# Convolution and leaky-ReLU feed-forward on one core: w_in fetched once, wider first transposes, fewer warm-ups, weight and x on two queues

## The chip, the cores and the metric

The kernel runs on one core of a Trainium2 chip. The metric is the device time of one execution in microseconds (us).

The profile names the engines PE (TensorE), PEld (its weight loads), DVE (VectorE), ACT (ScalarE), POOL (GpSimd) and SP (SyncE).

## The reference

```python
w = exp(weight - max); w = w / (sum(w) + 1e-9)            # 8 heads, 7 taps
out[b, s, h*24 + g] = sum_k w[h, k] * x_pad[b, s + k, h*24 + g]   # causal, 6 zeros ahead
h = out.reshape(32768, 192) @ moe_w_in                    # 192 x 2048
g = maximum(0.01 * h, h)
return g @ moe_w_out                                      # 2048 x 192, float32
```

## The kernel before

The 192 channels are three chunks of 64. Two batch rows lie side by side in the partitions (e = 0 in 0 to 63, e = 1 in 64 to 127), so the kernel keeps each weight that multiplies them in both halves. The work goes in groups: the first eight have 256 columns, the others 512. A group is convolved ("yt"), multiplied by w_in into PSUM ("ph", the first product), passed through leaky ReLU by ScalarE ("g"), and multiplied by w_out ("po" or "acc", the second product). The second product of a group runs one group later, so group 0 has no second product beside it.

The first 1024 columns of x do not take the usual path through DMA transposes, whose load and transpose take a median of 3.2 and 3.9 us from issue to landing in this kernel's profile. They are loaded in four quarters and transposed on TensorE: quarter 0 comes as float32 over the sync queue (`x_nat`), is cast, transposed into PSUM, the memory that this kernel's matmuls write ("ptr"), and evacuated, that is copied out, into `xt`; quarters 1 and 2 (`x_rows`) come over GpSimd's queue.

```python
def load_w_in(n, e):                       # six transfers: 3 pieces x 2 halves
    fs = slice(pieces[n] * 128, pieces[n + 1] * 128)
    nc.gpsimd.dma_start(out=w_in[n][e * CH : (e + 1) * CH],
                        in_=moe_w_in[:, fs].rearrange("(c p) f -> p c f", p=CH))
...
load_w_in(0, 0); make_identity(nc, ident); load_w_in(0, 1)
for e in range(2): load_w_in(1, e)
load_first(1)                              # x_rows, quarter 1
for e in range(2): load_w_in(2, e)
load_first(2)
nc.gpsimd.dma_start(out=w_out..., in_=moe_w_out...)
```

In group 0, chunks 0 and 1 are convolved on TensorE with diagonal weights (`diag`, each tap as a high and a low bfloat16 part, p = 0 and 1), chunk 2 on VectorE. In group 1, TensorE does chunk 0 and VectorE the other two. Idle TensorE time in the prologue is filled with matmuls on zeros ("warm").

## Time and profile before

| | |
|---|---|
| time, first three runs | 687.36 to 687.89 us, median 687.63 |
| span of the profiled run | 685.2 us (that run: 687.25 us) |
| first convolution on TensorE | 6.57 to 10.4 us |
| first product in earnest | from 10.95 us |
| second product | from 22.25 us |
| w_out's transfer | issued 9.64, landed 22.2 us |

Read it from the last row but one: TensorE waits for nothing from the second product's first matmul to the end (the waits view names no PE wait after 22.25 us, and PE is busy 200.00 of the 200 us from 200 to 400). The lines behind the table stand in the prediction.

### The profile page before, as it was taken

How to read it: one execution, taken by the hardware profiler on the slowest of the kernel's cores; microseconds unless marked ns; L12 is line 12 of the kernel's file. 1: busy time of each engine (PE TensorE's matmuls, PEld its weight loads, DVE VectorE, ACT ScalarE, POOL GpSimd, SP SyncE). 2: the span in 40 equal slices, each digit the busy share in tenths (PEclk: the TensorE clock that was granted, in tenths of full speed). 3: DMA queues.
4: the chain of work that ended last, by engine and by line, in shares of the span. 5: the costliest groups of instructions: out<-in, count | busy, mean ns of one | idle time of the engine just before them, and what ended most of it. 6: DMA issues, size and time to landing. Idle time of an engine off the chain costs nothing.

```text
span 685.2 us, 27404 instructions
## 1 busy us (share of the span) xinstructions
PE 679.2 (99%) x12572; PEld 466.0 (68%) x12572; DVE 483.7 (71%) x851; ACT 524.6 (77%) x623; POOL 147.5 (22%) x206
## 2 busy tenths in 40 slices
PE   9999999999999999999999999999999999999998
PEld 6899987666666666666666666666666666666667
DVE  6889668567687667786677786676876676876612
ACT  7888898777777778777777777777777778777781
POOL 7732222222102222022222022221122220000000
PEclk9999999999999999999999999999999999999999
DMA  9986658466566565575574565574665664321123
GB/s 155 112 96 95 83 70 107 44 76 89 84 87 76 55 83 85 82 95 68 55 91 80 87 87 67 60 95 75 90 81 61 72 91 75 72 55 34 34 49 93
DMA packets 211699, 53.88 MB, mean 79 GB/s; under 512 B 204288, under 2 KB 211200, under 8 KB 211584
## 3 DMA queue, kind: packets, MB, share of 16 engines
q0 software_dynamic: 99536, 14.76, 30.5%
q1 hardware_dynamic: 112048, 37.38, 26.9%
q8 instruction: 98, 1.61, 0.9%
q14 instruction: 17, 0.14, 0.1%
HBM read 29.88 MB, written 25.17 MB: 80 GB/s over the span
## 4 chain that ended last, share of the span: by engine, by line
PE 95%; DMA 2%; POOL 1%; ACT 1%; issue 0%; DVE 0%; POOLq 0%
PE ph L406 47%; PE acc L495 41%; PE po L432 7%; DMA w_out<-in_moe_w_out_dram 2%; ACT g L413 1%; POOL w_in L251 1%; POOL x_rows L125 0%; POOL sel L236 0%; DVE o_sb L543 0%; POOL ident masks.py:199 0%; POOL sel L234 0%; POOL ident masks.py:197 0%; PE ptr L151 0%; POOLq masks.py:199 0%; POOLq L642 0%
## 5 line engine op out<-in xcount | busy, mean ns | idle before, releaser
L413 ACT ACTIVATE g<-ph 128x1024 bf16<-128x1024 f32 x512 | 496.3, 1021 | 136.3 <-PE ph L406 135.8
L195 DVE SCALAR_TENSOR_TENSOR yt<-xt,wk,yt 128x512 bf16<-128x512 bf16 (+1 forms) x630 | 388.2, 696 | 0.2
L406 PE MATMUL ph<-yt,w_in 64*64 64x512 bf16 (+2 forms) x6048 | 377.9, 363 | 1.4 <-ACT g L413 0.7
L495 PE MATMUL acc<-g,w_out 64*64 64x512 bf16 x5184 | 316.5, 376 | 0.0
L406 PEld LDWEIGHTS <-w_in 64*64 64x64 bf16 (+1 forms) x6048 | 237.7, 129 | 98.9 <-issue 3.9
L495 PEld LDWEIGHTS <-w_out 64*64 64x64 bf16 x5184 | 166.3, 118 | 110.5
L80 POOL DMA_DIRECT2D x_bf<-in_x_dram x180 | 134.2, 779 | 412.3 <-DMA xt<-x_bf 408.4
L517 DVE STREAM_TRANSPOSE o_t<-acc 128x512 f32<-128x512 f32 x81 | 68.1, 884 | 170.0 <-PE acc L495 170.0
L432 PE MATMUL po<-w_out,g 64*128 64x192 bf16 (+1 forms) x1152 | 59.7, 243 | 0.2 <-DMA w_out<-in_moe_w_out_dram 0.2
L432 PEld LDWEIGHTS <-g 64*128 64x128 bf16 (+1 forms) x1152 | 55.2, 94 | 2.0 <-issue 0.8
L189 DVE TENSOR_SCALAR yt<-xt,wk 128x512 bf16<-128x512 bf16 (+1 forms) x105 | 29.4, 333 | 12.8 <-DMA xt<-x_bf 9.0
L505 ACT COPY junk<-junk 128x1 f32<-128x1 f32 x54 | 10.3, 191 | 3.9
L543 ACT COPY o_sb<-po 128x192 f32<-128x192 f32 x32 | 10.1, 320 | 1.5 <-PE po L432 0.2
L543 DVE COPY o_sb<-po 128x192 f32<-128x192 f32 x8 | 2.8, 356 | 6.8 <-PE po L432 3.8
L170 DVE COPY xt<-ptr 128x384 bf16<-128x384 bf16 x7 | 2.2, 353 | 6.0 <-PE ptr L158 3.2
L286 PE MATMUL warm<-zero 128*128 128x256 bf16 (+1 forms) x20 | 4.8, 404 | 1.1 <-DVE junk L231 1.1
L214 PE MATMUL acc<-xt,diag 64*64 64x256 bf16 x84 | 5.5, 288 | 0.0
L214 PEld LDWEIGHTS <-diag 64*64 64x64 bf16 x84 | 4.7, 115 | 0.9 <-DVE rsum L366 0.4
L129 POOL DMA_DIRECT2D x_half<-in_x_dram x6 | 4.3, 713 | 3.2 <-DMA w_in<-in_moe_w_in_dram 3.2
L251 POOL DMA_DIRECT2D w_in<-in_moe_w_in_dram x6 | 3.9, 656 | 0.0
L286 PEld LDWEIGHTS <-zero 128*128 128x128 bf16 x20 | 2.5, 136 | 2.1 <-DVE junk L231 1.1
L347 ACT ACTIVATE diag<-ident,whm 128x64 bf16<-128x64 bf16 x14 | 3.5, 336 | 0.0
(41 smaller groups left out, 18.8 us busy)
## 6 DMA issues: line engine op xcount, KB each, us to landing
out_dram<-o_t SPq DMA_DIRECT2D x108, 192.0 KB, 4.6
x_bf<-in_x_dram POOLq DMA_DIRECT2D x180, 64.0 KB, 3.2
out_dram<-o_sb SPq DMA_DIRECT2D x16, 192.0 KB, 3.0
xt<-x_bf SPq DMA_TRANSPOSE x90, 3.9
w_in<-in_moe_w_in_dram POOLq DMA_DIRECT2D x4, 192.0 KB, 5.4
w_in<-in_moe_w_in_dram POOLq DMA_DIRECT2D x2, 384.0 KB, 8.5
w_out<-in_moe_w_out_dram POOLq DMA_DIRECT2D x1, 768.0 KB, 12.6
out_dram<-o_sb SPq DMA_DIRECT2D x8, 96.0 KB, 1.9
```

The source lines that it names most:

```text
L80: nc.gpsimd.dma_start(out=t[:, c, :, e, :], in_=src[2 * rp + e, :, :, c * CH : (c + 1) * CH],)
L189: lambda s=src, d=dst, c=c: nc.vector.tensor_scalar_mul(d, s, wk[:, c, 0:1])
L195: lambda s=src, d=dst, c=c, k=k: nc.vector.scalar_tensor_tensor(out=d, in0=s, scalar=wk[:, c, k : k + 1], in1=d, op0=mybir.AluOpType.mult, ...
L214: lambda k=k, p=p, a=a, e=e, ps=ps: nc.tensor.matmul(out=acc[ps, :T], lhsT=diag[c][ps, p, k, :], rhs=xt[0][ps, c, a : a + T], start=(k == ...
L251: nc.gpsimd.dma_start(out=w_in[n][e * CH : (e + 1) * CH], in_=moe_w_in[:, fs].rearrange("(c p) f -> p c f", p=CH),)
L406: nc.tensor.matmul(out=ph[m : m + M, e, i * T : (i + 1) * T], lhsT=w_in_of(f, ps, c, m, m + M), rhs=y[ps, c, t0 : t0 + T], start=(c == 0), ...
L413: act = nc.scalar.activation(out=g[blk][:, nf * u : nf * (u + 1), :, t0 : t0 + T], in_=ph.rearrange("p e (i t) -> p i e t", i=nf), func=my ...
L432: return nc.tensor.matmul(out=po[m], lhsT=g[b][ps, fc, e, s * 128 : (s + 1) * 128], rhs=w_out[ps, fc, :], start=start, stop=stop,)
L495: ins = nc.tensor.matmul(out=acc2[gi, r][e * CH : (e + 1) * CH, 0:T], lhsT=w_out_of(ps, fc, r), rhs=g[b][ps, fc, e, t0 : t0 + T], start=fi ...
L505: seal = nc.scalar.copy(out=junk, in_=junk)
L517: nc.vector.transpose(out=osb[gi, 0][:, 0 : T // GB, :, r], in_=acc2.pop((gi, r))[:, 0:T].rearrange("p (j k) -> p j k", k=GB),)
L543: ins = copy(out=o_sb[:, n % 2, :], in_=po.pop(n))
```

## The change

Its intent is a shorter prologue. w_in is fetched once: 128 of its 192 rows land over all partitions, the other 64 in the lower half, and VectorE copies what the other half lacks (`spread_down`, `spread_up`). Chunk 2 of group 0 goes to TensorE too, with input and output halves crossed, so that its matmuls run beside those of the others. The first transposes take all 128 partitions. The weight is issued from ScalarE's queue so that x goes first on the sync queue. The casts of quarter 0 are shared between ScalarE and VectorE, as its evacuations were before. Of the warm-ups, nine of 256 columns between the weight's matmuls and the convolution become one of 256 and one of 512, and the nine of 256 and one of 128 at the start become six of 512.

```diff
-    NPEC = 2
+    NPEC = 3
...
+        t = psum_o.tile([128, HS, NCH, 128], BF16, name="ptr", tag="po")   # one PSUM tile, was two
+        for s in range(HS):
+            for c in range(NCH):
+                if q == 0:
+                    nc.tensor.transpose(out=t[:, s, c, :], in_=x_half[q][:, c, s, :, :]..., identity=ident)
...
-    nc.sync.dma_start(out=w9[:, 0:K], in_=weight)
+    nc.scalar.dma_start(out=w9[:, 0:K], in_=weight)
...
+    def load_w_in(n, rows):
+        ps, slot = ((0, 128), 0) if rows == 0 else ((0, CH), 2)
+        nc.gpsimd.dma_start(out=w_in[n][ps[0] : ps[1], slot],
+                            in_=moe_w_in[rows : rows + ps[1], n * WF : (n + 1) * WF])
+    def spread_down(n):
+        nc.vector.tensor_copy(out=w_in[n][0:CH, 1, :], in_=w_in[n][CH:128, 0, :])
+    def spread_up(n):
+        nc.vector.tensor_copy(out=w_in[n][CH:128, 1:3, :], in_=w_in[n][0:CH, 0:3:2, :])
...
-    warm(9)
-    warm(1, 128)
+    warm(6, ST)
...
-    warm(6)
+    warm(1)
...
-    warm(3)
+    warm(1, ST)
...
-    for e in range(2):
-        cast_first(0, e, nc.scalar.copy)
+    cast_first(0, 0, nc.scalar.copy)
+    cast_first(0, 1, nc.vector.tensor_copy)
...
+    run(pe_0[:K])
+    run(pe_0[K:], pe_2[:K])
+    evac_0(act_scale)
+    run(pe_1[:K], pe_2[K:])
+    evac_2(nc.vector.tensor_scalar_mul)
+    run(pe_1[K:])
+    evac_1(act_scale)
...
-                    evac_y(act_scale)          # group 1's TensorE chunk: ScalarE, at once
+                evac_0(nc.vector.tensor_scalar_mul)   # now VectorE, at the end of group 0
```

More of the change, by code (lines that the diff above doesn't have):

```diff
@@ L2 @@
 from contextlib import ExitStack
+from itertools import zip_longest
 import concourse.bass as bass
@@ L142, in transpose_first @@
     def transpose_first(q):
-        ts = [
-            psum_o.tile([128, HS, NCH, CH], BF16, name=f"ptr{i}", tag="po") for i in range(2)
-        ]
-        for s in range(HS):
-            for c in range(NCH):
-                for i in range(2):
-                    ps = slice(i * CH, (i + 1) * CH)
-                    if q in x_half:
+        if q == 3:
+            ts = [
+                psum_o.tile([128, HS, NCH, CH], BF16, name=f"ptr{i}", tag="po")
+                for i in range(2)
+            ]
+            for s in range(HS):
+                for c in range(NCH):
+                    for i in range(2):
+                        ps = slice(i * CH, (i + 1) * CH)
                         nc.tensor.transpose(
@@ L155, in transpose_first @@
                         )
-                        continue
-                    for e in range(2):
-                        nc.tensor.transpose(
-                            out=ts[i][e * CH : (e + 1) * CH, s, c, :],
-                            in_=x_rows[q][ps, e, s, c * CH : (c + 1) * CH],
-                            identity=ident[ps, ps],
-                        )
-        ptr[q] = ts
-    def evac_first(q, *copies):
-        dst = xt[0][:, :, HALO + q * HT : HALO + (q + 1) * HT].rearrange(
-            "p c (s i k) -> p i s c k", s=HS, i=2
-        )
-        for i, t in enumerate(ptr.pop(q)):
-            copies[i](out=dst[:, i], in_=t)
+            ptr[q] = ts
+            return
+        t = psum_o.tile([128, HS, NCH, 128], BF16, name="ptr", tag="po")
+        for s in range(HS):
+            for c in range(NCH):
+                if q == 0:
+                    nc.tensor.transpose(
+                        out=t[:, s, c, :],
+                        in_=x_half[q][:, c, s, :, :].rearrange("p e k -> p (e k)"),
+                        identity=ident,
+                    )
+                    continue
+                for e in range(2):
+                    nc.tensor.transpose(
+                        out=t[e * CH : (e + 1) * CH, s, c, :],
+                        in_=x_rows[q][:, e, s, c * CH : (c + 1) * CH],
+                        identity=ident,
+                    )
+        ptr[q] = t
+    def evac_first(q, *copies):
+        dst = xt[0][:, :, HALO + q * HT : HALO + (q + 1) * HT]
+        t = ptr.pop(q)
+        if q == 3:
+            dst = dst.rearrange("p c (s i k) -> p i s c k", s=HS, i=2)
+            for i in range(2):
+                copies[i](out=dst[:, i], in_=t[i])
+            return
+        dst = dst.rearrange("p c (s k) -> p s c k", s=HS)
+        for s in range(HS):
+            copies[s](out=dst[:, s], in_=t[:, s])
     yt = {}
@@ L200, in conv_jobs, with pe_conv_jobs @@
         return jobs
-    def pe_conv_jobs(grp, c, parts=(0, 1)):
+    def pe_conv_jobs(grp, c, parts=(0, 1), cross=False):
         blk, t0, T = grp
@@ L210, in pe_conv_jobs @@
                 a = BASE + k + blk * ST + t0
+                both = []
                 for e in range(2):
                     ps = slice(e * CH, (e + 1) * CH)
-                    jobs.append(
-                        lambda k=k, p=p, a=a, e=e, ps=ps: nc.tensor.matmul(
-                            out=acc[ps, :T], lhsT=diag[c][ps, p, k, :],
+                    to = slice((e ^ cross) * CH, ((e ^ cross) + 1) * CH)
+                    both.append(
+                        lambda k=k, p=p, a=a, ps=ps, to=to: nc.tensor.matmul(
+                            out=acc[to, :T], lhsT=diag[c][ps, p, k, :],
                             rhs=xt[0][ps, c, a : a + T],
@@ L220, in pe_conv_jobs, with evac, run @@
                     )
-        return jobs, lambda scale: scale(yt[blk][:, c, t0 : t0 + T], acc[:, :T], rsum[:, c, :])
+                jobs.append(both)
+        def evac(scale):
+            if blk not in yt:
+                yt[blk] = yt_pool.tile([128, NCH, ST], BF16, name="yt")
+            y = yt[blk][:, c, t0 : t0 + T]
+            if not cross:
+                scale(y, acc[:, :T], rsum[:, c, :])
+                return
+            for e in range(2):
+                ps = slice(e * CH, (e + 1) * CH)
+                frm = slice((1 - e) * CH, (2 - e) * CH)
+                scale(y[ps], acc[frm, :T], rsum[frm, c, :])
+        return jobs, evac
+    def run(*lists):
+        for slots in zip_longest(*lists, fillvalue=()):
+            for both in slots:
+                for job in both:
+                    job()
     w9 = const_pool.tile([H, K + 1], FP32, name="w9")
-    nc.sync.dma_start(out=w9[:, 0:K], in_=weight)
+    nc.scalar.dma_start(out=w9[:, 0:K], in_=weight)
     load_first(0)
-    zero = const_pool.tile([128, HT], BF16, name="zero")
-    nc.vector.memset(zero, 0.0)
+    ones = nc.const_aps.tensor(1.0, [128, ST], BF16)
     junk = const_pool.tile([128, 1], FP32)
@@ L240, with w_in_of @@
         )
-    pieces = (0, NFC // 4, NFC // 2, NFC)
-    w_in = [
-        const_pool.tile([128, NCH, (b - a) * 128], BF16, name=f"w_in{a}")
-        for a, b in zip(pieces[:-1], pieces[1:])
-    ]
-    def load_w_in(n, e):
-        fs = slice(pieces[n] * 128, pieces[n + 1] * 128)
+    NPW = 2
+    WF = F // NPW
+    w_in = [const_pool.tile([128, NCH, WF], BF16, name=f"w_in{n}") for n in range(NPW)]
+    def load_w_in(n, rows):
+        ps, slot = ((0, 128), 0) if rows == 0 else ((0, CH), 2)
         nc.gpsimd.dma_start(
-            out=w_in[n][e * CH : (e + 1) * CH],
-            in_=moe_w_in[:, fs].rearrange("(c p) f -> p c f", p=CH),
-        )
-    def w_in_of(f, ps, c, m0, m1):
-        n = max(n for n in range(3) if pieces[n] <= f)
-        a = (f // RUN * RUN - pieces[n]) * 128 + f % RUN
-        return w_in[n][ps, c, a + m0 * RUN : a - f % RUN + m1 * RUN : RUN]
+            out=w_in[n][ps[0] : ps[1], slot],
+            in_=moe_w_in[rows : rows + ps[1], n * WF : (n + 1) * WF],
+        )
+    def spread_down(n):
+        nc.vector.tensor_copy(out=w_in[n][0:CH, 1, :], in_=w_in[n][CH:128, 0, :])
+    def spread_up(n):
+        nc.vector.tensor_copy(out=w_in[n][CH:128, 1:3, :], in_=w_in[n][0:CH, 0:3:2, :])
+    def w_in_of(f, e, c, m0, m1):
+        n, f = divmod(f, NFC // NPW)
+        slot = c if c == 2 else c ^ e
+        a = f // RUN * RUN * 128 + f % RUN
+        return w_in[n][
+            e * CH : (e + 1) * CH, slot, a + m0 * RUN : a - f % RUN + m1 * RUN : RUN
+        ]
     load_w_in(0, 0)
@@ L263 @@
     make_identity(nc, ident)
-    load_w_in(0, 1)
-    for e in range(2):
-        load_w_in(1, e)
+    load_w_in(0, 128)
     load_first(1)
-    for e in range(2):
-        load_w_in(2, e)
+    for rows in (0, 128):
+        load_w_in(1, rows)
     load_first(2)
@@ L286, in warm @@
             nc.tensor.matmul(
-                out=wa[:, 0, 0:cols], lhsT=zero[:, 0:128], rhs=zero[:, 0:cols],
+                out=wa[:, 0, 0:cols], lhsT=ones[:, 0:128], rhs=ones[:, 0:cols],
                 start=True, stop=True,
@@ L312 @@
     nc.vector.tensor_add(ident2, ident[:, 0:CH], ident[:, CH:128])
-    warm(9)
-    warm(1, 128)
+    warm(6, ST)
     wps = psum_h.tile([128, 2, ST], FP32, name="wps", tag="ph")
     wps_hm = wps[:, 0, 0 : NCH * 2 * (K + 1)].rearrange("p (c q k) -> p c q k", c=NCH, q=2)
-    wps_l = psum_o.tile([128, NCH, K + 1], FP32, name="wps_l", tag="po")
+    wps_l = wa[:, 1, 0 : NCH * (K + 1)].rearrange("p (c k) -> p c k", c=NCH)
     def select(out, parts):
@@ L350, in diag_each @@
             )
-    for p in range(2):
-        diag_wide(0, p, K)
-    for e in range(2):
-        cast_first(0, e, nc.scalar.copy)
-    diag_each(1, 1, range(4))
-    transpose_first(0)
-    warm(3)
-    wraw = const_pool.tile([128, NCH, K + 1], FP32, name="wraw")
-    nc.vector.tensor_add(wraw, whm[:, :, 0], whm[:, :, 1])
-    nc.vector.tensor_add(wraw, wps_l, wraw)
-    rsum = const_pool.tile([128, NCH, 1], FP32)
-    nc.vector.tensor_scalar_add(rsum, wraw[:, :, K : K + 1], 1e-9)
-    evac_first(0, nc.vector.tensor_copy, nc.scalar.copy)
+    diag_wide(0, 0, K)
+    diag_each(1, 1, range(2))
+    transpose_first(0)
+    warm(1, ST)
+    evac_first(0, nc.scalar.copy, nc.vector.tensor_copy)
+    diag_wide(0, 1, K)
+    for p in range(2):
+        diag_wide(2, p, K)
+    spread_down(0)
+    rsum = const_pool.tile([128, NCH, 1], FP32)
+    wml = const_pool.tile([128, NCH, K + 1], FP32, name="wml")
+    nc.vector.tensor_add(wml, wps_l, whm[:, :, 1])
+    nc.vector.scalar_tensor_tensor(
+        out=rsum, in0=wml[:, :, K:], scalar=1e-9, in1=whm[:, :, 0, K:],
+        op0=mybir.AluOpType.add, op1=mybir.AluOpType.add,
+    )
     nc.vector.reciprocal(rsum, rsum)
-    wk = const_pool.tile([128, NCH, K], FP32, name="wk")
-    nc.vector.tensor_mul(wk, wraw[:, :, 0:K], rsum.to_broadcast([128, NCH, K]))
-    diag_each(1, 1, range(4, K))
+    diag_each(1, 1, range(2, K))
     diag_each(1, 0, range(K))
+    spread_up(0)
     def act_scale(out, in_, scale):
@@ L375, in act_scale @@
         )
-    for job in conv_jobs(groups[0], range(NPEC, NCH)):
-        job()
-    for c in range(NPEC):
-        pe_jobs, evac_y = pe_conv_jobs(groups[0], c, (c, 1 - c))
-        for job in pe_jobs:
-            job()
-        evac_y(act_scale)
+    pe_0, evac_0 = pe_conv_jobs(groups[0], 0)
+    pe_2, evac_2 = pe_conv_jobs(groups[0], 2, cross=True)
+    pe_1, evac_1 = pe_conv_jobs(groups[0], 1, (1, 0))
+    run(pe_0[:K])
[5 more added lines that the diff above has]
+    evac_1(act_scale)
+    wk = const_pool.tile([128, NCH, K], FP32, name="wk")
+    nc.vector.tensor_add(wk, whm[:, :, 0, 0:K], wml[:, :, 0:K])
+    nc.vector.tensor_mul(wk, wk, rsum.to_broadcast([128, NCH, K]))
     g, po, acc2, osb, seal = {}, {}, {}, {}, None
@@ L407, in mm1 @@
                             out=ph[m : m + M, e, i * T : (i + 1) * T],
-                            lhsT=w_in_of(f, ps, c, m, m + M),
+                            lhsT=w_in_of(f, e, c, m, m + M),
                             rhs=y[ps, c, t0 : t0 + T],
@@ L579 @@
                     evac_first(1, nc.vector.tensor_copy, nc.vector.tensor_copy)
-                    pe_ahead, evac_y = pe_conv_jobs(groups[1], 0)
-                    ahead = conv_jobs(groups[1], range(1, NCH))
+                    spread_down(1)
+                    spread_up(1)
+                    ahead = conv_jobs(groups[1], (1, 2))
                     per = len(ahead)
                 if i == 0 and u == 3:
-                    for job in pe_ahead:
-                        job()
-                    evac_y(act_scale)
-                if i == 0 and u == 6:
+                    pe_0, evac_0 = pe_conv_jobs(groups[1], 0)
+                    run(pe_0)
+                if i == 0 and u == 5:
                     transpose_first(2)
```

## The prediction

> **What bounds the kernel now.** I read the page's busy shares first, then the chain that ended last in its first 45 us, then the timeline of the first 32 us, then the waits.
>
> ```profile
> PE 679.2 (99%) x12572; PEld 466.0 (68%) x12572; DVE 483.7 (71%) x851; ACT 524.6 (77%) x623; POOL 147.5 (22%) x206
> ```
>
> TensorE is busy 99% of the span of 685.2 us. The windows view gives it 200.00 of the 200 us from 200 to 400, and the waits view shows no PE wait after 32 us. The change touches nothing in that long part: it has the same matmuls, and w_in's columns are read with the same stride from another slot. So only the start can move, and what I have to find is when the dense part begins. The chain tells when:
>
> ```profile
> 9.64 12.56 DMA w_out<-in_moe_w_out_dram
> 22.20 0.04 issue
> 22.25 1.50 PE po L432 x32
> ```
>
> From 22.25 us the second product (po) starts and TensorE never stops again. The chain blames w_out's transfer for all of 9.64 to 22.20. That is true only of who came last. The waits view says what it cost:
>
> ```profile
> PE po L432 <- DMA w_out<-in_moe_w_out_dram: 0.2, 1, 0.2
> ```
>
> The columns are the total, the count and the longest in us: 0.2 us once. PE had finished its work before that at 22.08. So a second chain, nearly as long, runs beside the transfer. The timeline shows it (start, busy time, what):
>
> ```profile
> 3.85 1.06 ACT L135 CAST x_half<-x_nat 128x384 bf16<-128x384 f32 x2 [1.10 <-DMA x_nat<-in_x_dram]
> ...
> 6.57 3.82 PE L214 MATMUL acc<-xt,diag 64*64 64x256 bf16 x56
> ...
> 10.43 0.47 ACT L373 ACTIVATE yt<-acc,rsum 128x256 bf16<-128x256 f32 x1 [1.06 <-PE acc L214]
> 10.95 1.28 PE L406 MATMUL ph<-yt,w_in 64*128 64x256 bf16 x20 [0.34 <-ACT yt L373]
> ...
> 11.73 3.90 ACT L413 ACTIVATE g<-ph 128x1024 bf16<-128x1024 f32 x4 [0.83 <-PE ph L406]
> ...
> 14.50 1.72 PE L214 MATMUL acc<-xt,diag 64*64 64x256 bf16 x28
> ...
> 17.09 6.04 ACT L413 ACTIVATE g<-ph 128x1024 bf16<-128x1024 f32 x6 [0.36 <-PE ph L406]
> ```
>
> x lands at 3.85, is cast, transposed and evacuated; TensorE does the first convolution from 6.57; ScalarE scales its last part until 10.90; the first product starts in earnest at 10.95. In this first group there is no second product to fill TensorE, so ScalarE's activation of about 1.0 us per step sets the pace: four (11.73 to 15.63), a hole while TensorE does the next convolution (to 17.09), and four more to about 21.1, after which the last first-product step ends at 22.08. **From 10.95 to 22.08 is 11.13 us of a fixed chain.** Call the start of the first product S: the dense part begins at S + 11.13, or when w_out lands, whichever is later.
>
> [...] In the trace an issue on the sync queue is 0.41 to 0.45 us, so splitting weight and x may bring x forward by that. [...] Now all six w_in transfers go to 64 partitions; from 4 to 6 us, the windows view shows the DMA engines 0.89 busy moving 107 GB/s, against 195 to 211 later. [...] ten warm-up matmuls (2432 columns) take 2.21 us, 1.1 columns per ns, and the convolution's starts come about 0.14 us apart until 7.4 us and about 0.05 apart from 8 us on, although the granted clock reads 1.00 throughout. [...] The one-source multiply agrees: 306 ns for 256 columns and 339 for 512.
>
> **The change part by part.**
>
> w_in once. Before, six transfers of 192 to 384 KB bring 1536 KB; now four (256, 128, 256, 128) bring 768 KB. Ahead of w_out's end on the GpSimd queue lay 1536 + 384 (x_rows) + 768 = 2688 KB; now 1920. Adding the windows' bytes from 4 us: 0.21 MB by 6, 0.47 by 8, 0.81 by 10, 1.20 by 12, 1.62 by 14, 2.01 by 16. 1920 KB (1.97 MB) are reached at about 16, so I estimate that w_out lands at 16 to 17.5 instead of 22.2. That gains only its 0.17 us of wait.
>
> The copies. VectorE gets two per piece, of 1024 and 2048 columns on 64 partitions; from the two points above I estimate 0.4 and 0.65 us, 2.1 us in all. The first pair needs w_in's first 384 KB; the same bytes landed at 8.45 before (issued 3.14, 5.3 to landing), so I take 8.0 to 8.5. It is followed by the scaling of chunk 2, two half-width ops of some 0.4 us: 8.3 + 0.65 + 0.8 = 9.75. The second pair delays the next group's convolution.
>
> x. Queue split: 0.46 us earlier (1.27 to 0.81), so about 3.4 and 3.85 for the two halves. The casts (0.51 each) go side by side on ScalarE and VectorE rather than one after the other: both end near 4.3 rather than 4.91. Six full-width transposes replace twelve half-width: 0.5 us either way. VectorE does one wide diagonal multiply (0.6) before its evacuation instead of two. I get the evacuation at 5.4 (before 6.4) and the convolution at 5.5 (before 6.57). The weight's path gets slower: if ScalarE issues the weight's fetch (0.41) before its table load (1.28, from 0.80), the exponential moves from 2.35 to about 2.7, but the first diagonal then waits for VectorE's cast anyway.
>
> The first convolution. A third chunk goes from VectorE (0.48 + 3.09 us) to TensorE[...]. So there are still 28 steps of two or four matmuls. If the clock rises at 7.4 as before: seven pairs at 0.21 to 7.0, two quads to 7.4, twelve quads at about 0.12 to 8.9, seven pairs at 0.107 to 9.6; scaling 0.47; S = 10.2. If it rises early, ScalarE sets it: cast to 4.0, whm at 4.4, two diagonals at 0.25, evacuation 0.48, twelve diagonals at 0.25 to 8.4, two scalings at 0.47: S = 9.4. I take 9.95 between them, **1.0 us earlier than 10.95**.
>
> The fixed chain. Scaling group 1's TensorE chunk moves from ScalarE to VectorE. No gain: the hole from 15.63 to 17.09 is TensorE's convolution (14.50 to 16.22) plus the next first-product step, and both remain. VectorE gets longer: its evacuation and convolution took 12.84 to 18.74, S + 1.89 to S + 7.79; add the second copies (1.05) and the scaling (0.4): S + 9.25. Group 1's first product began at S + 9.3, with about 0.25 us of slack behind it. It just fits.
>
> Sum: dense part at 9.95 + 11.13 = 21.1 rather than 22.25, 1.15 us less: 687.63 - 1.15 = 686.5.
>
> **The rivals.** (a) w_out is the bound, as the chain has it: then the dense part would start at about 17, and the time would be some 682. Against it: PE was 0.17 us short of not waiting, and ScalarE's activations can't be pulled forward. (b) VectorE's new copies become the wait, at the first group (w_in lands late, the copy of it stands ahead of rsum in VectorE's order) or the second (S + 9.25 grows by half a microsecond[...]): 687.0 to 687.6. For it: the margin is 0.25 us. Against: w_in's queue is shorter. (c) With fewer warm-ups the array is still slow through the convolution: 28 steps at 0.21 is 5.9 us, S = 12, time 688.5. For it: sixteen 256-column warm-ups go, six of them just before the transposes. Against: six of 512 columns stay and start earlier, from a constant that GpSimd has ready at 0.4 us.
>
> **Range and chances.** I give the sum's own scatter (S between 9.4 and 10.25) 60%, rival b 20%, c 10%, and 10% to more gain than I see, such as an early clock with an early x. That makes 685.5 to 687.6 the range. Two per cent is 13.8 us, more than the whole 22.25 us start could well lose or gain, so within 2% is all but certain.
>
> **What would show it.** The first convolution matmul at 5.5 us; first product at 9.95; first po matmul at 21.1 with no wait for w_out, which lands before 18; the same TensorE work after that. Wrong would be: po before 19 (rival a); the first group-1 product waiting for VectorE's scaling of yt (b); convolution steps at 0.2 us beyond 8 us (c); or any PE wait after 32 us.

## The result, and the profile after

The changed kernel took 687.34 us (median of six runs, 686.26 to 687.57) against 688.21 us (687.36 to 689.00) for the kernel before in the same rounds, which is 0.87 us less. Ratios and their 95% intervals are given from the fast runs of both kernels; they are not quite the ratio of the medians quoted. Here the ratio is 0.9986, with an interval of 0.9973 to 0.9999. By the record's limit of 2% this counts as the same time; that the difference is real rests on its coming again in after_again.

The span of the profiled run, however, is longer than before: 685.8 us against 685.2. The page's first line differs little from the one before:

```profile
PE 679.7 (99%) x12559; PEld 466.5 (68%) x12559; DVE 485.4 (71%) x853; ACT 523.6 (76%) x621; POOL 145.8 (21%) x204
```

The timeline of the changed kernel answers the lines of the prediction one by one (start, busy time, what, and in brackets the idle time before it and what ended that):

```profile
3.43 0.51 ACT L136 CAST x_half<-x_nat 128x384 bf16<-128x384 f32 x1 [0.21 <-DMA x_nat<-in_x_dram]
3.99 0.55 DVE L136 CAST x_half<-x_nat 128x384 bf16<-128x384 f32 x1
4.69 0.80 PE L164 MATMUL ptr<-ident,x_half 128*128 128x128 bf16 x6
5.52 0.48 ACT L188 COPY xt<-ptr 128x384 bf16<-128x384 bf16 x1 [0.25 <-PE ptr L164]
6.04 0.36 DVE L188 COPY xt<-ptr 128x384 bf16<-128x384 bf16 x1 [0.72 <-ACT xt L188]
6.45 5.05 PE L235 MATMUL acc<-xt,diag 64*64 64x256 bf16 x84 [0.53 <-DVE xt L188]
8.03 0.55 DVE L295 COPY w_in<-w_in 64x1024 bf16<-64x1024 bf16 x1
9.23 1.02 DVE L298 COPY w_in<-w_in 64x2048 bf16<-64x2048 bf16 x1
...
12.06 1.39 PE L460 MATMUL ph<-yt,w_in 64*128 64x256 bf16 x22 [0.33 <-ACT yt L421]
...
18.15 3.90 ACT L467 ACTIVATE g<-ph 128x1024 bf16<-128x1024 f32 x4 [1.41 <-PE ph L460]
...
21.47 1.50 PE L460 MATMUL ph<-yt,w_in 64*128 64x256 bf16 x24 [0.48 <-DVE yt L249]
22.81 1.49 PE L486 MATMUL po<-w_out,g 64*128 64x192 bf16 x32
```

x lands early and the casts run side by side, as meant. But the six wide transposes take 0.80 us where the twelve narrow ones took 0.50, the two evacuations follow one another, the convolution starts only 0.12 us earlier than before and takes 5.05 us, and the first product starts at 12.06 us, 1.1 us **later** than in the profile before. From there the second product follows after 10.75 us, with no wait for w_out (issued at 7.50, landed 9.6 us later). So this profile says "slower by 0.6 us" while the timed runs say "faster by 0.9". At least one of the two profiles had to be untypical; that is what the experiments began with.

### The profile page after: what moved, and what is told of

The parts are those of the page before. It is cut to its first block, busy times and chain, and to the rows that moved or that the text cites. A ratio compares the mean times of both kernels' runs of the same rounds, so it can differ in the third digit from the quotient of the medians.

```text
span 685.8 us, 27376 instructions
## 1 busy us (share of the span) xinstructions
PE 679.7 (99%) x12559; PEld 466.5 (68%) x12559; DVE 485.4 (71%) x853; ACT 523.6 (76%) x621; POOL 145.8 (21%) x204
## 4 chain that ended last, share of the span: by engine, by line
PE 96%; ACT 1%; DVE 1%; issue 0%; ACTq 0%
PE ph L460 47%; PE acc L549 41%; PE po L486 7%; ACT g L467 1%; PE acc L235 1%; DVE yt L213 1%; DVE xt L188 0%; ACT L337 0%; PE ptr L164 0%; DVE w_in L298 0%; ACTq L266 0%; PE warm L331 0%; ACT xt L188 0%; DVE yt L207 0%; ACT yt L421 0%
## 5 line engine op out<-in xcount | busy, mean ns | idle before, releaser
L597 ACT COPY o_sb<-po 128x192 f32<-128x192 f32 x32 | 10.2, 321 | 1.5 <-PE po L486 0.2
L235 PEld LDWEIGHTS <-diag 64*64 64x64 bf16 x112 | 6.4, 141 | 1.2 <-issue 0.7
L331 PE MATMUL warm<-const-bfloat16-1.0 128*128 128x512 bf16 (+2 forms) x9 | 4.0, 563 | 0.8 <-PEq L697 0.8
L126 POOL DMA_DIRECT2D x_rows<-in_x_dram x4 | 2.9, 742 | 0.0
```

What stands on the lines that cost most here:

```text
L235: lambda k=k, p=p, a=a, ps=ps, to=to: nc.tensor.matmul(out=acc[to, :T], lhsT=diag[c][ps, p, k, :], rhs=xt[0][ps, c, a : a + T], start=(k = ...
L597: ins = copy(out=o_sb[:, n % 2, :], in_=po.pop(n))
```

## The experiments

Fourteen profiles were taken: of the two kernels, each twice, and of ten variants. Two sums hold in all of them and make the rest readable. The columns: the first matmul of the convolution; the moment from which its matmuls take some 270 ns rather than some 420 ("fast from"); the first product in earnest after its last wait at the start; the second product's first matmul; the span; the span less the second product's start. All in us.

| profile | convolution | fast from | first product | second product | span | rest |
|---|---|---|---|---|---|---|
| before | 6.57 | 7.8 | 10.95 | 22.25 | 685.2 | 663.0 |
| before_again | 6.31 | start | 10.13 | 24.15 | 687.2 | 663.0 |
| before_few_warm | 6.28 | 8.4 | 11.11 | 23.54 | 686.5 | 663.0 |
| before_x_rows_first | 6.57 | 7.9 | 11.02 | 22.83 | 685.8 | 663.0 |
| before_w_in_once | 8.58 | 12.8 | 14.43 | 25.30 | 688.3 | 663.0 |
| before_w_in_once_2q | 6.96 | 8.7 | 12.22 | 23.20 | 686.2 | 663.0 |
| after | 6.45 | 10.2 | 12.06 | 22.81 | 685.8 | 663.0 |
| after_again | 6.42 | 9.4 | 11.66 | 22.62 | 685.6 | 663.0 |
| after_fill | 6.45 | 9.4 | 11.68 | 22.42 | 685.4 | 663.0 |
| after_warm_early | 6.51 | 9.2 | 11.64 | 22.38 | 685.4 | 663.0 |
| after_old_w_in | 6.45 | 9.6 | 11.74 | 22.42 | 685.4 | 663.0 |
| after_two_banks | 5.68 | start | 10.23 | 20.95 | 683.9 | 663.0 |
| after_w_in_twice | 6.17 | start | 10.19 | 28.24 | 691.2 | 663.0 |
| after_best | 5.62 | start | 9.59 | 20.56 | 683.6 | 663.0 |

The last column is the first sum: the dense part is the same 663.0 us everywhere, so the start of the second product explains the whole span. It also turns the spans for the timed runs into starts of the second product, to 0.1 us. For the kernel before, 36 such runs have a median span of 686.0 us (685.0 to 687.2), so 23.0 us for the second product; for the changed kernel 11 have 685.4 (684.5 to 685.8), so 22.4. The profile from which the prediction was made, 22.25, lies below all but one of the 36.

"Fast from" is a change of TensorE's granted clock. The trace keeps a list of clock records, each with a start and a length. In the ten profiles in which the change falls inside the first convolution, the first record starts within 0.05 us of the first fast matmul (7.76 us in before, 10.18 in after); in the four with "start" it starts at 3.68 to 4.64. Before it there is no record, and the windows view then says 1.00: in this stretch 1.00 means that nothing was recorded, not full speed. In the records of the fourteen traces every stretch between two changes was a whole multiple of 3.41 us (3.41, 6.83, 10.24, 662.19, 669.01, 675.84 and 679.25; 679.25 in before, 675.84 in after), and the moment of the first change differed from run to run (3.68 to 12.8 us).

The second sum is outside the span: time less span is 1.9 to 2.05 us in the six profiled runs built on the kernel before, and 1.7 to 1.85 us in the eight built on the changed one. Some 0.2 us of the change's 0.87 thus lies outside what the profile shows; no run says why.

The runs were on three chips. The kernel before had a median of 687.83 us, 687.52, and 688.3, so only ratios are compared.

### before_again: the kernel before, unchanged

> The kernel before, unchanged, for a second profile. Theory (the clock's rise is what differs between the profiles, and its moment shifts from run to run): the first convolution starts again at 6.57 us, but the moment at which its steps go from 0.2 to 0.1 us may lie elsewhere than 7.4 us, and first product and second product shift with it one for one; time within 0.1% of the kernel before, single runs spread over up to 1.5 us. Rival (the rise is fixed by the program): rise at 7.4 again, second product at 22.25 within 0.1.

Measured: 688.09 us (687.61 to 689.12), ratio 1.0002 (0.9988 to 1.0015). The profile did shift, as the theory has it, but not only for the reason it gave. The convolution started at 6.31 us, not 6.57, and its matmuls, by the view of one tile (count, then minimum, median and maximum in ns, then first and last start), were all fast:

```profile
L214 PE MATMUL acc<-xt,diag x56: 266/268/294, 6.3 to 9.3; 64*64 64x256 bf16 x56
```

The first product started 0.8 us earlier than in the first profile. Nevertheless the second product started 1.9 us later. The timeline shows why:

```profile
13.00 0.21 PE L158 MATMUL ptr<-ident,x_rows 64*64 64x64 bf16 x1 [1.47 <-DMA x_rows<-in_x_dram]
13.47 0.38 PE L158 MATMUL ptr<-ident,x_rows 64*64 64x64 bf16 x23 [0.26 <-DMA x_rows<-in_x_dram]
...
15.47 3.07 PE L214 MATMUL acc<-xt,diag 64*64 64x256 bf16 x28
```

TensorE waited for x_rows, which stood behind four w_in transfers on GpSimd's queue, and after that hole the 28 matmuls of group 1's convolution took 3.07 us where they took 1.72 in the first profile. The windows view has the granted clock (the share of TensorE's full speed) of this second slow stretch: 0.72 from 14 to 16 us and 0.50 from 16 to 18; the trace's record runs from 14.88 for 3.41 us. In the first profile the transposes of x_rows had started at 12.28, about when it landed (issued at 5.8, landed 6.6 later), so no wait showed. The lesson for the prediction: a third chain, x_rows, ran level with the two that I had seen, and the profile I read was of a run in which it happened not to bite.

### after_again: the changed kernel, unchanged

> The changed kernel, unchanged. Ratio again about 0.9986 (0.9975 to 0.9995). Theory (rise shifts from run to run): convolution starts at 6.45 again, but its steps fall to 0.1 us at another moment than 10.1 us, and the second product starts between 21.0 and 23.3 us accordingly. Rival (fixed by the program): rise at 10.1, second product at 22.8 again - and then the profile would not explain why the median is 0.9 us lower than before.

Measured: 687.12 us (686.31 to 687.36) against 687.83, ratio 0.9985 (0.9972 to 0.9998). The gain repeats. The matmuls were slow until 9.4 us rather than 10.2, the first product started at 11.66 and the second at 22.62. In neither profile of the changed kernel does TensorE wait for a transfer.

### before_few_warm: the kernel before with the fewer warm-ups alone

```diff
-    warm(6)
+    warm(1)
...
-    warm(3)
+    warm(1)
```

> The kernel before with seven of its nine warm-ups between the weight's matmuls and the convolution taken out (6 to 1 and 3 to 1). Theory (fewer warm-ups put the clock's rise off): rise at 9.5 us or later, the 56 convolution matmuls take 5 us rather than 3.8, second product about 1.0 us later, time 0.6 to 1.2 us above the kernel before. Rival (the warm-ups do nothing for the time): within 0.3 us of the kernel before.

Measured: 687.96 us (687.28 to 688.43), ratio 0.9999 (0.9987 to 1.0012). The rival is nearer: the convolution was fast from 8.4 us, between the first profile's 7.8 and the changed kernel's 9.4 and 10.2, and the time did not change. (One profile each can't say more about the warm-ups, since before_again, unchanged, was fast from the start.) In this profile, too, TensorE waited for x_rows (1.16 and 0.23 us, at 13.66 and 14.10), so an earlier first product would have been of no use. The chain that ended last ran through yet another transfer, w_in's last piece, which landed at 17.83.

### after_fill: the changed kernel with the hole before its convolution filled

```diff
-    warm(1, ST)
+    warm(2, ST)
+    warm(1)
```

> The changed kernel with the hole of 0.5 us before its convolution filled by warm-ups (one of 512 columns becomes two and one of 256). Theory [...]: rise earlier than in the changed kernel on average, time 0.3 to 1.0 us below it. Rival [...]: within 0.3 us of the changed kernel. Convolution's start 6.45, unchanged, in both.

Measured: 687.03 us (686.18 to 687.64), ratio 0.9986 (0.9973 to 0.9998), and fast from 9.4 us as in after_again. The theory finds no support: in this profile the rise came no earlier without the hole, and the time is that of the changed kernel.

### before_x_rows_first: x_rows ahead of w_in's second piece

```diff
-    for e in range(2):
-        load_w_in(1, e)
     load_first(1)
+    for e in range(2):
+        load_w_in(1, e)
```

> The kernel before with the second piece of x (x_rows) issued ahead of w_in's second piece, nothing else. Theory (w_in's double traffic makes x_rows land at 12.3 to 14.1 us, and that sets the start of the dense part in most runs of the kernel before): x_rows lands by about 11.5 us, no TensorE wait for it, second product within 11.3 us of the first product's start, time 0.4 to 1.0 us below the kernel before. Rival (the gain comes from the convolution and the casts, not from w_in): within 0.2 us of the kernel before.

Measured: 687.60 us (687.23 to 688.23), ratio 1.0003 (0.9989 to 1.0017). TensorE no longer waited for x_rows, but for w_in, and the second product started at 22.83, when w_out (issued 9.2, landed 13.6 later) was there:

```profile
16.93 1.50 PE L406 MATMUL ph<-yt,w_in 64*128 64x256 bf16 x23 [0.32 <-DMA w_in<-in_moe_w_in_dram]
...
22.83 1.50 PE L432 MATMUL po<-w_out,g 64*128 64x192 bf16 x32
```

Reordering the queue moves the wait from one transfer to the next; what stands in it is too much. The theory's time was wrong because it looked at one transfer alone. In the first profile the chain went through w_out; the same view (start, length, what) of before_again, before_few_warm and this run has one other transfer of the same queue each:

```profile
5.76 7.66 DMA x_rows<-in_x_dram
7.09 10.74 DMA w_in<-in_moe_w_in_dram
7.09 9.80 DMA w_in<-in_moe_w_in_dram
```

In the profiles of the changed kernel that chain holds no transfer; it runs through the first convolution and VectorE's work.

### after_w_in_twice: the changed kernel with every w_in transfer doubled

```diff
+        nc.gpsimd.dma_start(
+            out=w_copy[ps[0] : ps[1], n],
+            in_=moe_w_in[rows : rows + ps[1], n * WF : (n + 1) * WF],
+        )
```

> The changed kernel with every w_in transfer issued a second time into a tile that nobody reads: the old traffic, everything else new. Theory (the traffic ahead of x_rows was the cost): x_rows lands at 12 us or later instead of about 9, w_out past 20, TensorE waits for x_rows in the profile, and most or all of the gain goes: 0.3 to 1.2 us above the changed kernel. Rival (traffic is hidden): within 0.2 us of the changed kernel.

Measured: 692.99 us (692.59 to 693.91), ratio 1.0082. The direction is the theory's, the size is more than five times as large, so this run is not the fair copy of the old traffic that I took it for. GpSimd itself had to wait before it could issue two of the doubled transfers, and the edit made these waits: the copy of w_in's last 64 rows goes into the same part of `w_copy` as the copy before it, and waited for that one to land (7.46 and 16.25 us):

```profile
7.74 0.54 POOL L295 DMA_DIRECT2D w_copy<-in_moe_w_in_dram  x1 [3.60 <-DMA w_copy<-in_moe_w_in_dram]
...
16.54 0.52 POOL L295 DMA_DIRECT2D w_copy<-in_moe_w_in_dram  x1 [5.18 <-DMA w_copy<-in_moe_w_in_dram]
```

w_out was issued at 18.50 instead of 7.50 and the second product started at 28.24. It shows how hard the prologue hangs on GpSimd's queue; it does not measure what the single fetch is worth.

### after_two_banks: the first transposes into two PSUM tiles

```diff
-        t = psum_o.tile([128, HS, NCH, 128], BF16, name="ptr", tag="po")
+        if q == 0:
+            t = [psum_o.tile([128, NCH, 128], BF16, name=f"ptr0{s}", tag="po") for s in range(HS)]
+        else:
+            t = psum_o.tile([128, HS, NCH, 128], BF16, name="ptr", tag="po")
...
-            copies[s](out=dst[:, s], in_=t[:, s])
+            copies[s](out=dst[:, s], in_=t[s] if q == 0 else t[:, s])
```

> The changed kernel with its first transposes going to two PSUM tiles instead of one. Theory (VectorE's evacuation waits for ScalarE's because both read one tile): both evacuations start at 5.5 us, the convolution at 6.05 instead of 6.45. What it is worth: if the slow clock sets the first product's start, the rise stays where it is and up to 0.4 us is gained with the earlier slow steps counting half: 0 to 0.3 us below the changed kernel. Rival (the wait is for something else): convolution still at 6.45.

Measured: 686.57 us (685.71 to 687.24), ratio 0.9987 (0.9974 to 0.9999). The evacuations now run together, as the theory has it:

```profile
5.18 0.46 ACT L194 COPY xt<-ptr 128x384 bf16<-128x384 bf16 x1
5.22 0.35 DVE L194 COPY xt<-ptr 128x384 bf16<-128x384 bf16 x1
5.68 3.40 PE L241 MATMUL acc<-xt,diag 64*64 64x256 bf16 x84 [0.29 <-ACT xt L194]
...
10.23 1.25 PE L466 MATMUL ph<-yt,w_in 64*128 64x256 bf16 x19 [0.20 <-DVE yt L260]
```

The changed kernel's single tile holds 1536 bytes a partition, and its VectorE copy waited 0.72 us with ScalarE's copy named as what ended the wait; with two tiles the wait is gone and the copies start 0.04 us apart. The kernel before had two tiles. So the wider transposes brought this wait in, and it cost about 0.4 us on the way to the convolution. In the time nothing of it can be seen: the ratio is that of the changed kernel, 0.9985 to 0.9986 in its own rounds.

The profiled run (685.71 us) was one with a fast convolution from its first matmul: 84 matmuls in 3.40 us against 5.05. In it the first product waited last for VectorE, whose copies of w_in and whose scalings of chunk 2 (9.18 to 10.18) had become the end of the chain. How much of the median is due to the two tiles and how much to such runs can't be told from five runs.

### after_warm_early: warm-ups from 3.6 us to the convolution

```diff
     select(wps_hm, slice(0, 2))
-    warm(1, 128)
-    select(wps_l, 2)
-    warm(1)
+    warm(3)
...
     transpose_first(0)
+    warm(1)
+    select(wps_l, 2)
     warm(1, ST)
+    warm(1, 128)
```

> The changed kernel with the third weight part's matmuls moved behind the transposes and the time from 3.6 to 6.4 us filled with warm-ups. Theory [...]: matmuls of 269 ns from 7 us at the latest, the 84 of the convolution take 3.1 to 3.8 us rather than 4.7 to 5.05, and then VectorE's copies and scalings (until about 11.3) set the first product: 0.3 to 0.7 us below the changed kernel. Rival (the rise does not follow from warm-ups): rise past 9 us again, same time within 0.2 us.

Measured: five runs of 686.19, 686.20, 686.21, 687.14 and 687.16 us, median 686.21, ratio 0.9988 (0.9975 to 1.0000). The profiled run was one of the two slower ones, with fast matmuls from 9.2 us only. So the rival is the nearer one: the ratio is that of the changed kernel. The times fall into two groups 0.95 us apart, but the spans less so (684.4, 684.4, 684.5, 684.9 and 685.4; the run of 687.16 spent 2.26 us outside its span of 684.9). The rise was seen in one profile only, so that the groups are early and late rises is not shown. The warm-ups did not bring the rise forward in that profile, and whether they make early rises more frequent can't be said from five runs.

### after_old_w_in: the change without its single fetch

The edit puts back the six transfers and drops the copies; all else of the change stays.

```diff
-    load_w_in(0, 0) ... load_w_in(0, 128) ... for rows in (0, 128): load_w_in(1, rows)
+    the six transfers of the kernel before, and its w_in_of
-    spread_down(0)
-    spread_up(0)
...
-                    spread_down(1)
-                    spread_up(1)
```

> The changed kernel with w_in fetched as before (six transfers, twice the bytes) and no copies on VectorE; all else of the change stays. Theory (single fetch is worth its place because x_rows and w_out then never hold TensorE up): x_rows lands at 12 to 14 us again and w_out past 20; in the profile a TensorE wait for one of them; time 0.3 to 1.1 us above the changed kernel. Rival (the copies cost what the traffic saves): within 0.3 us of the changed kernel, or below it, since VectorE has 2.7 us less to do.

Measured: 687.25 us (686.81 to 687.97) against 688.33, ratio 0.9984 (0.9972 to 0.9996). The rival is right in time: without the single fetch the gain is the same. In its profile x_rows was transposed at 13.06 without a wait, because the first product had started only at 11.74 (slow matmuls until 9.6 us) and the old traffic was just in time for that. With an early clock it would perhaps have met x_rows as before_again did; no profile shows it. Its fastest run, 686.81, is half a microsecond above the fastest of the changed kernel (686.26), and the spans of all runs fit this. Of 51 runs with the six transfers (this variant's five among them) none had a span below 685.0 us, so none started the second product before 22.0; in their five profiles w_out landed at 21.4 to 22.9. Of 32 runs of the changed kernel and its variants with the single fetch (with after_best, which fetches a third of w_in twice, and without after_w_in_twice), 16 lay below 685.0, three of them among the changed kernel's own 11. So the old transfers seem to set a floor at about 22 us, which the single fetch removes and which only the better runs would notice. These runs are from three chips, and 10 runs of the fetch alone did not go below it either, so the floor is likely, not shown.

### before_w_in_once: the single fetch alone

The edit takes the new w_in code into the kernel before, with the first pair of copies behind chunk 2's convolution on VectorE.

```diff
     for job in conv_jobs(groups[0], range(NPEC, NCH)):
         job()
+    spread_down(0)
+    spread_up(0)
```

> The kernel before with the single fetch of w_in and VectorE's copies alone (the first pair after chunk 2's convolution on VectorE). Theory: x_rows lands near 9 us and w_out by 17.5, no TensorE wait for either; the first product is held by the copies until 11.3 to 11.9 us; second product at 22.2 to 22.9 in every clock state, so 0.2 to 0.9 us below the kernel before. Rival (the single fetch gives nothing by itself): within 0.2 us of the kernel before or slower.

Measured: 688.74 us, from 687.39 to 690.31 with three of six runs above 689.4; ratio 1.0007 (0.9991 to 1.0023). There was no wait for x_rows or w_out, but a new one at the very start of the profiled run, that of 690.31:

```profile
3.75 0.51 ACT L135 CAST x_half<-x_nat 128x384 bf16<-128x384 f32 x1 [1.00 <-DMA x_nat<-in_x_dram]
6.69 0.51 ACT L135 CAST x_half<-x_nat 128x384 bf16<-128x384 f32 x1 [2.43 <-DMA x_nat<-in_x_dram]
```

The second half of x landed 4.9 us after its issue instead of 2.6 (one profile; that the two other runs above 689.4 have the same cause was not seen). It had been issued at about 1.7 us, beside w_in's first transfer, which now goes to all 128 partitions and is issued from 1.84. The whole convolution moved to 8.58.

### before_w_in_once_2q: the single fetch, with the weight on ScalarE's queue

```diff
-    nc.sync.dma_start(out=w9[:, 0:K], in_=weight)
+    nc.scalar.dma_start(out=w9[:, 0:K], in_=weight)
```

> The single fetch of w_in alone, as in before_w_in_once, with the weight on ScalarE's queue so that x is issued 0.46 us earlier. Theory (in before_w_in_once x's second half was caught behind w_in's first, now wider, transfer, and the two parts of the change need one another): both halves of x land 2.6 us after issue, by 3.9 us, no cast waits at 6.7; no TensorE wait for x_rows or w_out; second product 10.9 us after the first product's start, at 22.2 to 22.9; no runs near 690; median 1.0 to 1.8 us below that of before_w_in_once as a ratio to the kernel before (ratio 0.9980 to 0.9995 instead of 1.0007). Rival (the single fetch costs more on VectorE than it saves in any case): ratio 1.0000 or above with x landing early.

Measured: 688.06 us (687.81 to 688.19, four runs), ratio 0.9994 (0.9980 to 1.0009). Of the theory, the first half holds: both halves of x landed 2.7 us after issue, no cast waited at 6.7, no run was near 690 and the spread fell to 0.4 us. The second half does not: what the single fetch saves in waits, its copies seem to cost on VectorE in this place. TensorE waited for the second copy:

```profile
12.22 1.50 PE L413 MATMUL ph<-yt,w_in 64*128 64x256 bf16 x23 [0.99 <-DVE w_in L258]
```

So the second product, at 23.20, was later than foretold (22.2 to 22.9). The ratio lies at the upper edge of what the theory expected, and its interval includes 1.

### after_best: what the runs pointed to, together

```diff
     (two PSUM tiles, as in after_two_banks; the third weight part behind the transposes)
+        for e in range(2):       # w_in's last 64 rows fetched into both halves
+            nc.gpsimd.dma_start(out=w_in[n][e * CH : (e + 1) * CH, 2], in_=moe_w_in[128 : 128 + CH, fs])
...
-        nc.vector.tensor_copy(out=w_in[n][CH:128, 1:3, :], in_=w_in[n][0:CH, 0:3:2, :])
+        nc.vector.tensor_copy(out=w_in[n][CH:128, 1, :], in_=w_in[n][0:CH, 0, :])
...
-                if i == 0 and u == 3:
-                    run(pe_0)
+                if i == 0 and 2 <= u <= 5:
+                    run(pe_0[4 * (u - 2) : 4 * (u - 1)])
+                if i == 0 and u == 5:
+                    evac_0(act_scale)
```

> The changed kernel with: two PSUM tiles for the first transposes; the third weight part's matmuls behind the transposes; w_in's last 64 rows fetched into both halves so that VectorE's second copy halves; group 1's TensorE convolution spread over four steps so that ScalarE never waits 1.4 us for it, and its scaling back on ScalarE. Theory: the first product starts 0.3 to 0.5 us earlier than in the changed kernel at the same clock, the hole of 1.41 us between two activations is gone, and the second product follows the first product's start by 9.9 to 10.2 us rather than 10.7: 1.0 to 1.6 us below the changed kernel. Rival (the chain is held elsewhere, for instance by VectorE's convolution of group 1): no more than 0.5 us below it.

Measured: 685.51 us (median of six; 685.35 to 686.13 and one run of 687.83) against 688.33, ratio 0.9966 (0.9952 to 0.9980). In time the theory holds: the changed kernel itself was not in this lot, but with its ratio elsewhere of 0.9985 this is some 1.3 us below it. The profiled run had a fast convolution from the start, as after_two_banks had, and its first product began at 9.59, earlier by 0.6 us at the same clock. The other half of the theory fails: the second product followed 10.97 us later, not 9.9 to 10.2. The hole of 1.41 us did not vanish; it fell into pieces:

```profile
13.67 1.02 ACT L476 ACTIVATE g<-ph 128x1024 bf16<-128x1024 f32 x1 [0.32 <-PE ph L469]
15.01 1.02 ACT L476 ACTIVATE g<-ph 128x1024 bf16<-128x1024 f32 x1 [0.31 <-PE ph L469]
16.34 1.02 ACT L476 ACTIVATE g<-ph 128x1024 bf16<-128x1024 f32 x1 [0.31 <-PE ph L469]
```

A step with four pairs of convolution matmuls takes TensorE 1.34 us (13.67 to 15.01), more than ScalarE's 1.02. There TensorE is the bound, and spreading its work changes nothing. The gain came from the start of the chain; and four of the six runs have the profiled run's span of 683.6 us, so the early clock seems to have come often. Why it did was not found.

## Why the prediction was right or wrong

The number was right: 686.5 us predicted with a range of 685.5 to 687.6, and 687.34 measured; 1.13 us of gain forecast, 0.87 found. The way to it was right in its frame and wrong in its largest term. That the gain came out near is luck: the second product was foretold for 21.1 us and starts at about 22.4, some 1.3 later, but the kernel before starts it at about 23.0 and not at the 22.25 of the one profile, and the 0.2 us outside the span were not foreseen at all.

**The dense part** (right). "TensorE never stops again" from the second product on: 663.0 us in all profiles. That w_out's earlier landing would gain next to nothing by itself also held (before_w_in_once_2q: landed at 17.4, second product at 23.20); rival (a), 682 us, is out. The 0.17 us named for it was small: PE's 22.08 is the modelled end of its last matmuls, and in before_again, where w_out had landed 1.2 us before, the second product followed the start of the step before it by 0.65 us, against 1.02 in the first profile. The wait was thus nearer to 0.37 us.

**The start of the first product, "S = 9.95", 1.0 us earlier** (wrong). It was 12.06 and 11.66 in the two profiles of the changed kernel. The step that failed is the working of x and of the convolution:
- "The evacuation at 5.4" ended at 6.40. x landed as foretold to 0.1 us (3.41 and 3.96), and the casts ended 0.2 us late (4.54). But "0.5 us either way" for the transposes was 0.80, at the same slow rate at which the narrow ones had taken 0.50: the wide ones start 0.107 us apart, the narrow ones ran in pairs 0.052 apart. And the two evacuations were serial, because both read one PSUM tile, which cost another 0.4; after_two_banks shows this by undoing it.
- "If the clock rises at 7.4 as before": it rose at 9.4 and 10.2. The convolution's 84 matmuls took 4.7 and 5.05 us against 3.40 when fast. This is rival (c) in part, but not for its reason: taking warm-ups out of the kernel before, and adding them to the changed one, moved neither the time nor, in the profiles, the rise in the way that I expected; that warm-ups set the rise was my assumption, and no run shows it. In three profiles of its variants the matmuls were fast from the first. (The prediction's count of warm-ups was off by one: seventeen of 256 columns go, and seven of 512 come.)
- "0.4 and 0.65 us" for the first copies were 0.55 and 1.02 (0.42 and 0.69 for the second pair; the two points that it names, 306 and 339 ns, give 0.54, so that 0.65 was an estimate that no measurement bore out; the second pair is the better measure, with 0.27 us more for 1024 columns more), and chunk 2's scalings 1.0 rather than 0.8. With the fast clock this ends the chain: 10.23 in after_two_banks, not 9.4.

So S is not earlier: 10.19 to 10.23 against 10.13 with a fast convolution, and 11.66 to 12.06 against 10.95 with a slow start, though there the rise itself came at different moments (9.4 and 10.2 against 7.8).

**"From 10.95 to 22.08 is 11.13 us of a fixed chain"** (nearly). From first to second product it was 10.68 to 10.97 us in the changed kernel's family wherever no transfer interfered. In the changed kernel VectorE's copies, its convolution and its scaling of group 1's chunk 0 end this chain: TensorE waited 0.48 and 0.70 us for that scaling. That wait is the sign which the prediction named for rival (b), at the second group: "it just fits" missed by 0.5 to 0.7 us. The scaling's end itself was nearly as foretold, S + 9.35 and S + 9.56 against S + 9.25; TensorE was ready for it earlier than S + 9.3.

**What the prediction lacked.** It took one profile of the kernel before for the kernel before. That profile (22.25, in a run of 687.25 us) was one of its best: the medians of the rounds, 687.5 to 688.3, lie up to 1.1 us above it, and the spans of the timed runs put the second product at 23.0 in the middle. In two of the next three profiles with its six transfers (before_again, before_few_warm, before_x_rows_first) TensorE waited for x_rows, and in each of the four the chain that ended last went through a transfer of GpSimd's queue: w_out, x_rows and twice w_in. The prediction saw one of these three. The spans leave some 0.6 us of gain between the medians (0.8 between the means) inside the span, with the 0.2 us outside it.

These transfers are tied to one another. In the traces of the two kernels (before and after), this program's GpSimd transfers signal eight semaphores in turn, 106 to 113, and from the ninth on each issue waits for the semaphore of the transfer eight before it. In the kernel before, w_out is the eleventh and waits for w_in's third transfer: that landed at 9.35 and 10.71 us (before and before_again), and w_out was issued at 9.64 and 11.00. With the single fetch it is the ninth and waits for w_in's first transfer, which landed at 6.27 us; it was issued at 7.50, behind the eighth, without a wait. So not only w_in's bytes but the number of its transfers held w_out back, which the prediction's sum of bytes leaves out.

**Which part of the change carries it** is settled in part. The single fetch is not what the gain of the median hangs on: all the rest without it gives 0.9984, the fetch alone 1.0007, and with the queues split 0.9994. Fewer warm-ups alone give 0.9999. What remains is the group of x's earlier landing, the shared casts, the wide transposes, the third chunk on TensorE and the moved scaling; these were not taken apart, and no part was shown to give the 0.9 us alone. That all the rest comes to the same without the single fetch is not explained: in its one profile the old transfers were just in time. Also open: what decides when the matmuls become fast, at 3.7 to 12.8 us in the fourteen profiles, and the 0.2 us outside the span.

## What to carry to other kernels

When a prologue of 20 us feeds a dense part, take several profiles of the old kernel before judging a change of 0.1%, and read the spans of all timed runs, because two or three chains of nearly equal length may take turns at being last. When an evacuation is to be split over two engines, give each its own PSUM tile: here the second copy waited 0.72 us for the first with one tile, and started 0.04 us after it with two. A transfer that is made wider or earlier should be checked against the small load that the first instruction waits for: here x's second half landed 4.9 us after its issue when it went out at 1.7 us, beside w_in's first transfer, and 2.7 us after it when it went out 0.4 us earlier (before_w_in_once and before_w_in_once_2q, one profile each).
